# Routing three of the last token tiles inside the attention loop, and the fourth among the last merges

## The chip, the cores and the metric

The kernel runs on one core of one Trainium2 chip. The time is that of one execution on the device, in microseconds; the figure given is the median of several runs. Five engines work beside each other, each through its own queue in order: TensorE (PE, with its weight loads shown as PEld), VectorE (DVE), ScalarE (ACT), GpSimd (POOL) and SyncE (SP), which here issues most transfers.

## The reference

Three stages follow each other on 1152 tokens (2 sequences of 576) of 512 features:

```python
scores = 0.125 * q @ k.T                      # 2 x 8 heads, 576 x 576, head_dim 64
kth = np.partition(scores, -32)[..., -32]     # only the 32 largest of a row count
attn = softmax(where(scores >= kth, scores, -1e9))
x = (attn @ v)                                # -> 1152 x 512

logits = x @ w_gate                           # 8 experts
e = argmax(logits); gate = softmax(logits)[e]
# token i is the counts[e]-th of its expert; dropped if counts[e] >= capacity (288)
y = relu(x_e @ w1[e]) @ w2[e]                 # per expert
x = gate * y

h = x @ w_in
out = (h * clip(h + 3, 0, 6) / 6) @ w_out     # 512 -> 2048 -> 512
```

A token's place in its expert's list depends on all tokens before it, so the routing of a tile of 128 tokens needs the choices of the earlier tiles.

## The kernel before, in words

The tokens are cut into nine tiles of 128 (0 to 8), each with eight heads: 72 units `u`, eight to a tile. `in_steps` runs a software pipeline over 73 steps `i`; in one step each unit is at another stage. `STEP`, a string of letters, is the order written out by hand in which the stages are put into the queues: R is the first-round maxima of unit i+1 (`round1`, eight MAX8 on VectorE) interleaved with the merge of unit i-3 (`merge`, the 32 largest, seven dependent operations); G is `rest` (norm of half a tile, gate logits, routing, and the `judge` operations on POOL); L is `round2` of unit i-2 (L360); X, C and B are `excess` (POOL, L348), `cut_excess` (ScalarE, L353) and `drop_excess` (POOL, L356), which prepare what `round2` reads; S, Z and M are `shift` (POOL, L385), `shift_rest` (ScalarE) and `below` (ScalarE, L394); T is `ptr` (five pairs of transposing matmuls on TensorE, L408 and L409), E the exponential `expo` (ScalarE), A the product `attv` (TensorE, L426). `part` and `mask` are VectorE's versions of `shift` and `below`, used behind the loop. Buffers of `excess` (s2) are three, of the transposed scores in PSUM (`pt`) one.

Routing has parts: `pick` (L465 to L470, five VectorE operations), `weigh` (an exponential), `count` (small matmuls that number the tokens of an expert, then a copy to SBUF), and `weight + place` (L486 to L494, seven VectorE operations), whose result `dest` is the row in the DRAM tensor `xs`. `ROUTES` says which tiles are routed together, in which step, and how many steps lie between two sends: tiles 0 to 3 in step 41, sent every sixth step; tiles 4 to 7 in step 71. `pick` is put into step `at`, the placing into step `at + 1`. The second group's placing is put in once in step 72 and once more behind the loop. `scatter` scales a tile's rows on ScalarE (L518) and sends them by an indirect DMA from POOL's queue (L140).

The first expert's 192 rows do not wait for all tokens: rows of tiles 0 to 6 are read back from `xs` by `load_first` (two DMAs on SP's queue, L188 and L189) and turned by TensorE (`x_rows`, L166), and those of tiles 7 and 8 are added by a matmul with a matrix of ones and zeros (`x_pick`, L173, with the matrix `pick0` that VectorE makes) into the same two PSUM banks, which are then copied to `xe0`. Behind that come eight experts (L819) and the feed-forward stage. `keep_warm` is a number of matmuls on zeros whose result is not used (L566).

Of the kernel before, what the change touches and what calls it, by code (L numbers as in the profile page):

```python
# [8 lines left out]
F32 = mybir.dt.float32  # L9
# [9 lines left out]
P = 128  # L19
# [3 lines left out]
NT = 9  # L23
NU = NT * H
# [20 lines left out]
KW = 11  # L45
FILL = 4
MIX = {1: (0, 0), 3: (0, 1), 5: (0, 2), 7: (0, 3), 11: (1, 0), 15: (1, 1), 19: (1, 2), 23: (1, 3)}
ROUTES = ((0, 4, 41, 6), (4, 8, 71, 1))
VS = D + 9
VC = 96  # L50
MC = 96
# [6 lines left out]
def topk_attention_moe_ffn_kernel(ctx, tc, qT, kT, vx, vT, wg, w1, w2, w_in, w_out, out, cap):  # L58
    nc = tc.nc
# [18 lines left out]
    def forward(fast):  # L78
# [79 lines left out]
        def x_copy(xp, g, x):  # L158
            nc.vector.tensor_copy(x[:, 2 * g:2 * g + 2, :W], xp[:, :, :W])

        def x_rows(xp):
            for g in range(2):
                for i in range(2):
                    ks = slice((2 * g + i) * P, (2 * g + i + 1) * P)
                    for r, r0, n in ((x0, 0, P), (x0b, P, W - P)):
                        nc.tensor.matmul(xp[g][:, i, r0:r0 + n], r[:, ks], ident[:n, :n], is_transpose=True,  # L166
                                         start=False, stop=False)

        def x_pick(xp, xg, t, start=False, x=None):
            for g in range(2):  # L170
                for i in range(2):
                    ks = slice((2 * g + i) * P, (2 * g + i + 1) * P)
                    nc.tensor.matmul(xp[g][:, i], xg[:, ks], pick0[t], start=start and i == 0,  # L173
                                     stop=x is not None and i == 1)
                if x is not None:
                    x_copy(xp[g], g, x)
# [14 lines left out]
        with ExitStack() as actx:  # L191
# [137 lines left out]
            def interleave(*chains):  # L329
                chains = [list(c) for c in chains]  # L330
                n = max([1] + [len(c) for c in chains])
                for i in range(n):
                    for ops in chains:
                        for f in ops[i * len(ops) // n:(i + 1) * len(ops) // n]:
                            f()
# [22 lines left out]
            def round2(u):  # L358
                t, h = divmod(u, H)
                nc.vector.max(lists[t % 2][:, h, NCK], st2.pop(u))  # L360
# [200 lines left out]
            def in_steps():  # L561
                wm = ps_t.tile([P, 8, P], F32, name="pt").rearrange("p a b -> p (a b)")[:, :512]

                def keep_warm(n, out):
                    for _ in range(n):
                        nc.tensor.matmul(out, dummy[:, :P], dummy, start=True, stop=True)  # L566

                def rest(i):
                    t, h = divmod(i - 4, H)
                    tn, hn = divmod(i - LAG, H)  # L570
                    if t >= 0 and h == H - 1:
                        judge(t)
                    interleave(norm(tn, hn - 3, hn + 1) if tn >= 0 and hn % 4 == 3 else [],
                               gate(tn - 1) if tn > 0 and hn == 0 else [],
                               *[routes[at][3 * (i - at)] for _, _, at, _ in ROUTES if i in (at, at + 1)])

                def issue(u):
                    if u % 2 == 0:
                        if u % H == 0 and 2 < u // H + 2 < NT:
                            load_q(u // H + 2)  # L580
                        scores(u, u + 1)

                routes = {}
                sent = 0
                blocks = {"X": (0, excess), "C": (1, cut_excess), "B": (1, drop_excess), "L": (2, round2), "S": (3, shift),
                          "Z": (3, shift_rest), "M": (3, below), "T": (4, ptr), "E": (4, expo), "A": (5, attv)}
                keep_warm(KW, wm)
                issue(0)
                for u in range(2):
                    fetch(u)  # L590
                interleave(round1(0))
                issue(2)
                fetch(2)
                for i in range(NU + 1):
                    for a, b, at, _ in ROUTES:
                        if i == at:
                            routes[at] = route(a, b)
                    if i == 16:
                        for name in stream[:2]:
                            load_w(name)  # L600
                        clear_rows(zero)
                    for o in STEP:
                        if o == "R":
                            interleave(round1(i + 1) if i + 1 < NU else [], merge(i - 3) if i >= 3 else [])
                        elif o == "G":
                            rest(i)
                        elif o == "F":
                            if i + 3 < NU:
                                fetch(i + 3)
                        elif o == "Q":  # L610
                            if i % 2 == 0 and i + 4 < NU:
                                issue(i + 4)
                            if i in MIX:
                                mix(*MIX[i])
                            if i < 4:
                                keep_warm(FILL, wm)
                        elif o == "V":
                            if i - 1 in MIX:
                                mixed(*MIX[i - 1])
                        elif 0 <= i - blocks[o][0] < NU:  # L620
                            blocks[o][1](i - blocks[o][0])
                    for a, b, at, gap in ROUTES:
                        if i == at:
                            routes[at][1]()
                            routes[at][2]()
                        n, r = divmod(i - at - 2, gap)
                        if r == 0 and 0 <= n < b - a:
                            scatter(a + n)
                            sent = a + n + 1
                mine = {t: big.tile([P, 1], F32, name=f"mine{t}") for t in xg_last}  # L630

                def pick(t):
                    nc.vector.scalar_tensor_tensor(mine[t], pos[:, t, 0:1], 1.0, oh[:, t, 0:1], op0=OP.add, op1=OP.mult)
                    nc.vector.tensor_scalar(pick0[t], slot1, mine[t], None, op0=OP.is_equal)

                u = NU - 1
                round2(u)
                interleave(merge(u - 1), merge(u), norm(NT - 1, 0, 4), routes[NU - 1][3])
                spare = ps_s.tile([P, 2, 512], F32, name="ps")[:, 0]
                warm = lambda n: keep_warm(n, spare)  # L640
                send = lambda t: scatter(t) if t >= sent else None
                for f, *args in ((ptr, u - 2), (expo, u - 2), (attv, u - 3), (send, 4), (send, 5), (attv, u - 2),
                                 (warm, 5), (part, u - 1), (below, u - 1), (part, u), (mask, u), (ptr, u - 1),
                                 (expo, u - 1), (send, 6), (load_first,), (scale, 7, xg_last[7]), (warm, 5), (ptr, u),
                                 (attv, u - 1), (pick, NT - 2), (expo, u), (judge, NT - 1), (warm, 1), (attv, u)):
                    f(*args)

                t = NT - 1
                banks = [pool.tile([P, 2, 512], F32, name=name)[:, 0, :2 * W].rearrange("p (a w) -> p a w", a=2)
                         for pool, name in ((ps_s, "ps"), (ps_t, "pt"))]  # L650
                interleave(norm(t, 4, H))
                x_pick(banks, xg_last[NT - 2], NT - 2, True)
                interleave(gate(t))
                nc.scalar.copy(plain.rearrange("p (h d) -> p h d", d=D), x_tok[:, t, :, :D])
                route_now(t, NT, lambda pos, tot: [
                    lambda: nc.vector.scalar_tensor_tensor(mine[t], pos[:, 0, 0:1], 1.0, oh[:, t, 0:1], op0=OP.add,
                                                           op1=OP.mult),
                    lambda: nc.vector.tensor_scalar(pick0[t], slot1, mine[t], gates[:, t], op0=OP.is_equal,
                                                    op1=OP.mult),
                    *most(tot)])  # L660
                x_rows(banks)
                send_rows(NT - 2, xg_last[NT - 2])
                x_pick(banks, plain, t, False, xe0)
                warm(WARM[1])
                nc.scalar.activation(xg_last[t], plain, AF.Copy, scale=gates[:, t])
                send_rows(t, xg_last[t])
# [355 lines left out]
```

## Time and profile before

| | us |
|---|---|
| median of 3 runs | 641.39 (641.07 to 641.99) |
| profiled execution | 639.62 |
| its span in the trace | 637.8 |
| PE busy in the span | 609.8 (96%) |
| DVE busy | 375.5 (59%) |
| ACT busy | 360.3 (56%) |
| POOL busy | 311.3 (49%) |

The profile is of one execution. Times in its rows count from the start of the span. Busy shares over the whole span are means over stages with different limits: the attention loop until about 234 us, its tail until 254 us, the experts until 428 us, the feed-forward stage until the end.

### The profile page before, as it was taken

To read this page: it belongs to the slowest core of one execution; us is meant where nothing else is said; L and a number is where in the kernel's file an instruction comes from. 1 tells how busy PE (TensorE), PEld (TensorE's weight loads), DVE (VectorE), ACT (ScalarE), POOL (GpSimd) and SP (SyncE) were. 2 spreads that over 40 slices of the span, in tenths; PEclk is the share of its full clock that TensorE was granted. 3 is DMA by queue.
4 is the path that set the end of the run, shared out by engine and by line. 5 is a ranking of instruction groups with operands and counts; after the bars stand their busy time and mean duration, and the time that the engine had idled before them with its cause. 6 is when DMAs were issued, how large, how long until landed. Compare 5 with 4: busy or idle time off the path is not lost.

```text
span 637.8 us, 12077 instructions
## 1 busy us (share of the span) xinstructions
PE 609.8 (96%) x4096; PEld 549.2 (86%) x4096; DVE 375.5 (59%) x1765; ACT 360.3 (56%) x687; POOL 311.3 (49%) x380
## 2 busy tenths in 40 slices
PE   8999999999888879999999999999999999999994
PEld 4888889888777767999999999999999999999993
DVE  5999999999999994002333323427665664222220
ACT  5999999989999963121334334336555553242221
POOL 7999999979999953001244222124234322030001
PEclk9999999999999979999999999999999999999998
DMA  8549600100000002885889887422222310020001
GB/s 268 168 134 386 212 17 2 35 2 18 18 18 19 2 1 95 293 290 148 306 264 280 276 308 239 165 64 85 81 85 84 97 34 1 1 99 1 1 1 54
DMA packets 36598, 74.13 MB, mean 116 GB/s; under 512 B 4016, under 2 KB 12464, under 8 KB 36528
## 3 DMA queue, kind: packets, MB, share of 16 engines
q1 hardware_dynamic: 34800, 68.55, 32.7%
q0 software_dynamic: 1728, 4.72, 2.0%
q8 instruction: 34, 0.56, 0.3%
q14 instruction: 36, 0.29, 0.2%
HBM read 63.83 MB, written 9.44 MB: 115 GB/s over the span
## 4 chain that ended last, share of the span: by engine, by line
PE 52%; DVE 24%; issue 15%; POOL 6%; ACT 1%; DMA 1%; DVEq 0%; SPq 0%; POOLq 0%; ACTq 0%
PE hps L819 13%; PE yps L819 13%; PE h L916 8%; PE acc L930 7%; DVE lists L342 7%; DVE lists L360 5%; DVE l L369 4%; DVE tops L371 3%; PE av L426 2%; POOL s L356 2%; PE ps L321 2%; PE pt L408 2%; POOL out_dram L939 1%; PE pt L566 1%; PE mix L443 1%
## 5 line engine op out<-in xcount | busy, mean ns | idle before, releaser
L342 DVE MAX8 lists<-s 128x8 f32<-128x72 f32 x576 | 118.6, 220 | 4.1 <-ACT s L326 4.1
L426 PE MATMUL av<-vt,pts 128*128 128x96 f32 (+1 forms) x800 | 100.5, 275 | 0.0
L916 PE MATMUL h<-x2h,fw 128*128 128x384 f32 x384 | 98.3, 336 | 0.9 <-DVE x2l L837 0.9
L426 PEld LDWEIGHTS av<-vt,pts 128*128 128x128 f32 (+1 forms) x800 | 92.1, 184 | 2.1 <-issue 0.9
L356 POOL TENSOR_TENSOR s<-s,cut 128x576 f32<-128x576 f32 x72 | 92.0, 1277 | 3.6 <-ACT cut L353 3.5
L819 PE MATMUL yps<-hT,wslot 128*128 128x192 f32 x512 | 90.9, 326 | 0.0
L930 PE MATMUL acc<-fw,gh 128*128 128x512 f32 x288 | 89.6, 392 | 0.0
L348 POOL TENSOR_TENSOR s<-s,lists 128x576 f32<-128x576 f32 x72 | 83.6, 1162 | 6.1 <-DVE lists L342 3.8
L408 PE MATMUL pt<-ident,ub 128*128 128x128 f32 x360 | 72.6, 287 | 13.5 <-POOL ub L385 7.9
L819 PE MATMUL hps<-xe,wslot 128*128 128x192 f32 x512 | 84.6, 326 | 0.2 <-DVE sc L184 0.2
L819 PEld LDWEIGHTS hps<-xe,wslot 128*128 128x128 f32 x512 | 83.4, 190 | 0.7 <-issue 0.7
L819 PEld LDWEIGHTS yps<-hT,wslot 128*128 128x128 f32 x512 | 82.1, 190 | 1.2
L408 PEld LDWEIGHTS pt<-ident,ub 128*128 128x128 f32 x360 | 50.8, 141 | 33.6 <-POOL ub L385 16.4
L916 PEld LDWEIGHTS h<-x2h,fw 128*128 128x128 f32 x384 | 70.5, 188 | 5.1 <-DVE x2l L837 1.2
L409 PE MATMUL pt<-drop,lb 128*128 128x128 bf16 x360 | 65.7, 220 | 0.0
L916 PE MATMUL h<-x2l,fw 128*128 128x384 f32 x192 | 64.7, 337 | 0.0
L930 PEld LDWEIGHTS acc<-fw,gh 128*128 128x128 f32 x288 | 53.4, 188 | 9.0
L919 ACT ACTIVATE g<-h,three 128x384 f32<-128x384 f32 x48 | 27.9, 581 | 55.7 <-PE h L916 55.7
L920 DVE SCALAR_TENSOR_TENSOR g<-g,h 128x384 f32<-128x384 f32 x48 | 26.5, 551 | 54.3 <-ACT g L919 53.9
L394 ACT ACTIVATE lb<-s,tops 128x576 bf16<-128x576 f32 x71 | 55.0, 775 | 4.9 <-DVE tops L371 2.8
L924 DVE TENSOR_TENSOR gl<-g,gh 128x384 fp32r<-128x384 f32 x48 | 27.4, 571 | 51.0 <-ACT gh L923 51.0
L923 ACT CAST gh<-g 128x384 fp32r<-128x384 f32 x48 | 24.7, 515 | 57.5 <-PE acc L930 52.9
(393 smaller groups left out, 1057.2 us busy)
## 6 DMA issues: line engine op xcount, KB each, us to landing
wslot<-in_w_dram SPq DMA_DIRECT2D x15, 2048.0 KB, 9.3
raw<-in_w_in_dram SPq DMA_DIRECT2D x16, 512.0 KB, 5.0
raw<-in_w_out_dram SPq DMA_DIRECT2D x16, 512.0 KB, 3.6
xs<-x_tok SPq DMA_DIRECT2D x8, 576.0 KB, 13.1
vt<-in_vx_dram SPq DMA_DIRECT2D x8, 365.0 KB, 3.6
kt<-in_kT_dram SPq DMA_DIRECT2D x8, 288.0 KB, 4.5
vts<-in_vT_dram SPq DMA_DIRECT2D x8, 288.0 KB, 3.8
qt<-in_qT_dram SPq DMA_DIRECT2D x9, 256.0 KB, 4.2
```

The lines of the kernel that those rows point to most:

```text
L342: yield lambda c=c: nc.vector.max(lists[t % 2][:, h, c], st[u][:, c * CW:(c + 1) * CW])
L348: nc.gpsimd.tensor_tensor(s2, s, lists[t % 2][:, h, :NCK, KEEP:].to_broadcast([P, NCK, CW]), op=OP.subtract)
L356: nc.gpsimd.tensor_tensor(st2[u], st[u], cuts.pop(u), op=OP.subtract)
L360: nc.vector.max(lists[t % 2][:, h, NCK], st2.pop(u))
L394: nc.scalar.activation(lbufs[u % 2][:, :S], st.pop(u), AF.Relu, bias=tops[t][:, h, TOPK - 1:], scale=-1.0)
L408: nc.tensor.matmul(pt[:, c], ubufs[u % 2][:, cs], ident, is_transpose=True, start=True, stop=False)
L409: nc.tensor.matmul(pt[:, c], lbufs[u % 2][:, cs], drop, start=False, stop=True)
L426: nc.tensor.matmul(av[t, g][rows, h % 4], pts[:, c, cols], vt[b, h // 2][:, at:at + VC], start=c == 0, stop=c == 4)
L819: nc.tensor.matmul(out, wb[:, k], m[:, k], start=first and k == 0, stop=last and k == HP - 1)
L916: nc.tensor.matmul(h2, fw[f][:, 0, a, k * P:(k + 1) * P], (x2h, x2l)[b][:, k, c * CH:(c + 1) * CH], start=n == 0, stop=n == len(ops) - 1)
L919: nc.scalar.activation(g, h2, AF.Relu, bias=three)
L930: nc.tensor.matmul(acc[j], g[a][:, j * P:(j + 1) * P], fw[f][:, 1, b], start=f == 0 and n == 0, stop=f == NF - 1 and n == 2)
```

## The change

Tiles 4 to 6 are routed in step 63, their rows are sent in the steps 65, 66 and 67, and the read-back is put behind step 69. Tile 7 is routed alone behind the loop: its `pick` is interleaved with the merge of unit 71, the rest follows the last mask. The two last merges are no longer interleaved with each other. The row transposes move ahead of the last attention product and now clear the banks; both banks come from one PSUM tile. Two groups of five warming matmuls are gone, and so is the second placing.

```diff
-ROUTES = ((0, 4, 41, 6), (4, 8, 71, 1))
+ROUTES = ((0, 4, 41, 6), (4, 7, 63, 1))
+FIRST = 69
...
-        def x_rows(xp):
+        def x_rows(xp, start):
             for g in range(2):
                 for i in range(2):
                     ks = slice((2 * g + i) * P, (2 * g + i + 1) * P)
                     for r, r0, n in ((x0, 0, P), (x0b, P, W - P)):
                         nc.tensor.matmul(xp[g][:, i, r0:r0 + n], r[:, ks], ident[:n, :n], is_transpose=True,
-                                         start=False, stop=False)
-
-        def x_pick(xp, xg, t, start=False, x=None):
+                                         start=start and i == 0 and r0 == 0, stop=False)
+
+        def x_pick(xp, xg, t, x=None):
             for g in range(2):
                 for i in range(2):
                     ks = slice((2 * g + i) * P, (2 * g + i + 1) * P)
-                    nc.tensor.matmul(xp[g][:, i], xg[:, ks], pick0[t], start=start and i == 0,
+                    nc.tensor.matmul(xp[g][:, i], xg[:, ks], pick0[t], start=False,
                                      stop=x is not None and i == 1)
...
                         if r == 0 and 0 <= n < b - a:
                             scatter(a + n)
-                            sent = a + n + 1
+                    if i == FIRST:
+                        load_first()
...
-                u = NU - 1
-                round2(u)
-                interleave(merge(u - 1), merge(u), norm(NT - 1, 0, 4), routes[NU - 1][3])
-                spare = ps_s.tile([P, 2, 512], F32, name="ps")[:, 0]
-                warm = lambda n: keep_warm(n, spare)
-                send = lambda t: scatter(t) if t >= sent else None
-                for f, *args in ((ptr, u - 2), (expo, u - 2), (attv, u - 3), (send, 4), (send, 5), (attv, u - 2),
-                                 (warm, 5), (part, u - 1), (below, u - 1), (part, u), (mask, u), (ptr, u - 1),
-                                 (expo, u - 1), (send, 6), (load_first,), (scale, 7, xg_last[7]), (warm, 5), (ptr, u),
-                                 (attv, u - 1), (pick, NT - 2), (expo, u), (judge, NT - 1), (warm, 1), (attv, u)):
+                u, t = NU - 1, NT - 1
+                wm, xp = (ps_s.tile([P, 2, 512], F32, name="ps") for _ in range(2))
+                warm = lambda n: keep_warm(n, wm[:, 0])
+                banks = [xp[:, g, :2 * W].rearrange("p (a w) -> p a w", a=2) for g in range(2)]
+                pick_e, weigh, count, place, _ = route(t - 1, t)
+                interleave(merge(u - 1), norm(t, 0, 4))
+                for f in (shift, shift_rest, below):
+                    f(u - 1)
+                for f, *args in ((ptr, u - 2), (expo, u - 2), (attv, u - 3), (round2, u)):
                     f(*args)
-
-                t = NT - 1
-                banks = [pool.tile([P, 2, 512], F32, name=name)[:, 0, :2 * W].rearrange("p (a w) -> p a w", a=2)
-                         for pool, name in ((ps_s, "ps"), (ps_t, "pt"))]
+                interleave(merge(u), pick_e)
+                for f, *args in ((weigh,), (part, u), (mask, u), (ptr, u - 1), (expo, u - 1), (attv, u - 2), (count,),
+                                 (ptr, u)):
+                    f(*args)
+                interleave(place)
+                for f, *args in ((pick, t - 1), (expo, u), (attv, u - 1), (x_rows, banks, True), (scale, t - 1, xg_last[t - 1]),
+                                 (judge, t), (warm, 1), (attv, u)):
+                    f(*args)
                 interleave(norm(t, 4, H))
-                x_pick(banks, xg_last[NT - 2], NT - 2, True)
+                x_pick(banks, xg_last[t - 1], t - 1)
...
-                x_rows(banks)
                 send_rows(NT - 2, xg_last[NT - 2])
-                x_pick(banks, plain, t, False, xe0)
+                x_pick(banks, plain, t, xe0)
                 warm(WARM[1])
```

## Rows read from the trace of the kernel before

**Rows 1.** Stretches: start:end, length, busy PE, PEld, DVE, ACT, POOL, PEclk, DMA, GB/s.
```profile
220.00:230.00 10.00, 6.71 (x65) 6.15 (x65) 9.66 (x53) 7.78 (x13) 10.00 (x12) 1.00 0.01 2
230.00:240.00 10.00, 8.30 (x68) 7.71 (x68) 9.52 (x56) 5.45 (x10) 2.19 (x4) 0.66 0.00 0
...
254.40:427.60 173.20, 173.00 (x1081) 171.49 (x1081) 50.50 (x118) 55.56 (x142) 39.07 (x43) 1.00 0.74 242
427.60:637.80 210.20, 201.22 (x1008) 181.84 (x1008) 91.37 (x156) 84.99 (x156) 47.43 (x44) 0.99 0.15 47
```

**Rows 2.** Chain of work that ended last: start, length, what; 244 to 255 us.
```profile
244.27 2.72 DMA xs<-xg,dest
...
247.39 2.98 DMA wslot<-xs
...
250.41 0.73 PE ps L166 x3
...
254.41 10.64 PE hps L819 x64
```

**Rows 3.** Timeline, all engines: start, length, engine, line, operation [idle before <-releaser]; 231 to 252 us.
```profile
231.80 0.23 DVE L367 MAX8 tops<-lists 128x8 f32<-128x63 f32 x1
...
233.69 0.17 DVE L486 TENSOR_REDUCE gt<-el 128x4 f32<-128x32 f32 x1
...
234.76 1.41 DVE L360 MAX8 lists<-s 128x8 f32<-128x576 f32 x2
...
240.17 0.51 DVE L402 TENSOR_SCALAR lb<-s,tops 128x576 bf16<-128x576 f32 x1
...
243.44 0.14 PEld L408 LDWEIGHTS pt<-ident,ub 128*128 128x128 f32 x1 [0.27 <-ACT pts L415]
...
244.30 1.20 PEld L426 LDWEIGHTS av<-vt,pts 128*128 128x128 f32 x10
...
247.00 0.16 DVE L432 TENSOR_SCALAR rs<-av 128x4 f32<-128x4 f32 x1 [5.77 <-PE av L426]
...
249.81 0.38 DVE L658 TENSOR_SCALAR wslot<-wslot,mine,gates 128x192 f32<-128x192 f32 x1
...
251.99 0.62 PEld L173 LDWEIGHTS ps<-wslot 128*128 128x128 f32 x4
```

**Rows 4.** Timeline of POOL alone, 137 to 231 us.
```profile
137.18 0.32 POOL L377 TENSOR_TENSOR over<-lists 128x64 f32<-128x64 f32 x1
...
142.96 1.16 POOL L140 DMA_INDIRECT xs<-xg,dest  x1 [1.48 <-DVE tops L371]
...
198.57 1.27 POOL L356 TENSOR_TENSOR s<-s,cut 128x576 f32<-128x576 f32 x1
...
201.07 1.17 POOL L348 TENSOR_TENSOR s<-s,lists 128x576 f32<-128x576 f32 x1
...
209.60 1.16 POOL L348 TENSOR_TENSOR s<-s,lists 128x576 f32<-128x576 f32 x1
...
228.62 0.51 POOL L385 TENSOR_TENSOR ub<-tops,s 128x200 f32<-128x200 f32 x1
229.10 1.26 POOL L356 TENSOR_TENSOR s<-s,cut 128x576 f32<-128x576 f32 x1
```

**Rows 5.** Timeline of VectorE alone, 130 to 231 us.
```profile
130.87 1.12 DVE L466 TENSOR_TENSOR dl<-L,mx 128x32 f32<-128x32 f32 x1
...
136.15 1.10 DVE L491 TENSOR_SCALAR rd<-cm 128x4 f32<-128x4 f32 x1
...
203.99 0.76 DVE L360 MAX8 lists<-s 128x8 f32<-128x576 f32 x1 [0.29 <-POOL s L356]
206.83 0.76 DVE L360 MAX8 lists<-s 128x8 f32<-128x576 f32 x1
...
228.53 1.89 DVE L466 TENSOR_TENSOR dl<-L,mx 128x32 f32<-128x32 f32 x1
...
230.45 0.19 DVE L467 SCALAR_TENSOR_TENSOR cand<-dl,desc 128x32 f32<-128x32 f32 x1
```

More of the change, by code (lines that the diff above doesn't have):

```diff
@@ L583, in in_steps @@
                 routes = {}
-                sent = 0
                 blocks = {"X": (0, excess), "C": (1, cut_excess), "B": (1, drop_excess), "L": (2, round2), "S": (3, shift),
```

## The prediction

> **What bounds the kernel now.** First I read the busy times by stretch [rows 1]. From 254.40 us on the expert stage holds TensorE busy for 173.00 of 173.20 us, and in the feed-forward stage it is busy for 201.22 of 210.20 us, the drain at the end included: whatever moves the first expert matmul moves the end by as much. The change lies wholly before that matmul, so the question is when it starts; it starts at 254.41 [rows 2]. In the last part of the attention loop, 220 to 230 us, the tight engine is another one: POOL 10.00 of 10 us, VectorE 9.66, TensorE only 6.71 [rows 1].
>
> Second, the chain that ended last [rows 2]: the send of tile 6's rows leaves POOL at 244.27 and takes 2.72 us to land, the read-back takes 2.98 us more, at 250.41 the rows are in, and their transposes run until tile 8's own picks can start at 251.99 [rows 3]. Third, the tail in time order [rows 3]: the pick matrix of tile 8, the other input of those picks, was made by VectorE at 249.81 + 0.38 = 250.19. So the read-back chain is late by only 251.99 - 250.25 = 1.74 us against a parallel chain (last attention product, norm, gate, routing of tile 8) that the change leaves in place. That is all that the removal of the two transfers can give.
>
> **The change part by part.** I use two marks. T is the start of the second-round maximum of unit 70 (L360, step 72): 234.76 now [rows 3]. N is the start of the last norm: 247.00 now, T + 12.24 [rows 3].
>
> *Sends and read-back out of the tail.* The transfers then lie some 14 us ahead of their use (last send in step 67, read-back behind step 69; from the send's start to the rows' arrival it was 250.41 - 244.27 = 6.1 us [rows 2]). After N nothing else changes: pick matrix at N + 3.19, picks at N + 3.25, and from the picks to the first expert matmul 254.41 - 251.99 = 2.42 us as now. Gain at equal N: 1.74 us. Both PSUM banks now come from one tile; I take the copy of one bank and the matmuls of the other as independent, at nothing (if not, a copy of some 0.6 us is added).
>
> *Sends into the loop.* POOL is the bound there and has no idle time from 201.07 to 230.36. One send costs it 201.07 - (198.57 + 1.27) = 1.23 us, gap to gap [rows 4]; with the memset and gaps I take 1.25. Three in the steps 65, 66 and 67 cost 3.75 us, less only what slack POOL has. Each also needs a scaling on ScalarE ahead of it. In step 43, right after a routing, the first send waited 1.48 us for that scaling [rows 4]; the order of work in step 65 is the same, ScalarE's `below` waits for VectorE's merge, then come the exponential and the scaling. I count 1.15 us for the first send (bounds 0 and 1.48), nothing for the next two, which POOL reaches later than ScalarE does. On the other queues: SP holds only the read-back and then the expert weights, which wait for the tail anyway. On ScalarE three scalings lie beside a POOL step of 4.1 us.
>
> *Routing into the loop, step 63.* VectorE gets there at 203.99 - 0.29 = 203.70 [rows 5]. There are five operations in step 63 and seven in step 64. An undisturbed one takes 0.19 us and a gap of 0.03 (230.45 [rows 5]). Two kinds are not undisturbed: the subtraction `dl` (L466), which reads two tiles of SBUF, and `rd` (L491). `dl` took 1.12 us in step 41 and 1.89 us in step 71 [rows 5]; the second one began at 228.53, POOL operations began at 228.62 and at 229.10, and it ended at 230.42, when the last one was over at 229.10 + 1.26 and POOL had nothing to do [rows 4, 5]. So it did not get in between two POOL operations that followed each other. In step 63 POOL runs without a gap until it is starved: its next `excess` (step 64) may start only when VectorE's L360 of step 63 is through, for s2 has three buffers. From 201.07 and 2.84 us a step (three steps to 209.60 [rows 4]) POOL runs dry at 206.75. I take `dl` until then; three more operations give L360 at 207.45 instead of 203.99, and its end, 208.2, starts POOL again. Step 64: first round and merge are 206.83 - 203.99 - 0.75 = 2.08 us [rows 5], to 210.3; three operations to 210.9; `rd` until POOL's operation is over at 211.1 (in step 42 it took 1.10 us [rows 5]); three more, and L360 of step 64, which I call X, starts at 211.7, now 206.83. Bounds: with no such wait at all 203.70 + 1.05, + 0.75 + 2.08, + 1.4 = 209.0; with `dl` at the one-operation price 210.4; with TensorE late with the position counts, as in step 41, 212.2.
>
> The Trainium skill, "SBUF — State Buffer", section "Who interferes with whom", states that a VectorE instruction with two SBUF inputs and a GpSimd instruction that reads SBUF exclude each other, and that the one which issues first has the ports for its whole instruction. By that rule `dl` would wait for one POOL operation, and X would be the 210.4 of the second case; the 1.89 us of step 71 lies over two, so the trace agrees with the exclusion and not with the turn-taking.
>
> *What this makes of T.* POOL's `excess` of step 65 starts at X + 0.75. From there to the end of its last drop operation of the loop it has 229.10 + 1.26 - 209.60 = 20.76 us of gapless work now [rows 4]; with 3.75 and 1.15 added, T = X + 0.75 + 20.76 + 3.75 + 1.15 = X + 26.4 = 238.1. VectorE alone would be there earlier: from L360 of step 64 to T it needs 234.76 - 206.83 = 27.9 us now, but some 3.7 of these are the routing, of which it is rid. T is 3.35 us later than now. What leaves the loop in exchange is in these numbers: now VectorE does the routing in steps 71 and 72, which is why T comes 4.4 us after POOL's last operation.
>
> *The tail, T to N.* VectorE now runs two second rounds (1.41 us), both merges together with norm and a repeated placing, two shifts, a mask, until 240.68, T + 5.92 [rows 3]. After the change: second round 0.71, merge of 70 with norm 2.25 (a merge alone takes 233.69 - 231.80 = 1.89 us [rows 3]; what is put between its dependent steps adds little), second round 0.71, merge of 71 with tile 7's pick 2.1, mask 0.51 and a shift of about that length: T + 6.8. The last transposes `ptr` then start at T + 6.9 (now 243.44, T + 8.7, held by the exponential of unit 70 and by a TensorE at half clock in part of 230 to 240 us [rows 1, 3]). Behind them on TensorE: 0.86 us for themselves, 1.2 us for the product of unit 70 [rows 3], the row transposes that have moved here, 8/7 of 251.99 - 250.41 = 1.8 us [rows 2, 3], and 247.00 - 245.50 = 1.5 us for one warming matmul and the last product: N = T + 12.26. So what the two dropped groups of five warming matmuls and the shorter wait give, the row transposes take. I count 0 for the tail, bounds -0.5 and +1.0.
>
> *Sum.* +3.35 + 0.0 - 1.74 = +1.6 us. The profiled execution took 639.62 us, 1.82 around its span of 637.8, and lies 1.77 below the median of 641.39; I add the difference to either: 641.2 profiled, 643.0 as the median.
>
> **The rivals.**
>
> *One operation's wait (641.7).* `dl` gets in at the next boundary of POOL, 203.95, and the next two-input operations each at a boundary; L360 of step 63 is at 205.9, POOL is not starved there, X = 210.4, T = 236.8, +2.05 - 1.74 = +0.3. For it: `rd` of step 42 ended at 137.25 although POOL went on at 137.18 [rows 4, 5]. Against it: step 71's `dl`.
>
> *Covered after all (639.2, faster).* The routing slips in without a wait and the first scaling is ready before POOL has done its step: X = 209.0, T = 209.75 + 20.76 + 3.75 = 234.26, 0.5 earlier than now; -0.5 - 1.74 = -2.2. It is decided by whether POOL's `excess` of step 65 starts before 210 us. For it: VectorE waits 0.29 us for POOL at 203.99, so there is a little room, and the repeated placing is gone. Against it: the waits of steps 41, 42, 43 and 71, every routing that the trace shows.
>
> *Half clock in the tail (645.9).* The granted clock was 0.66 on average in 230 to 240 us, so it was at the lower of its two levels (1.2 instead of 2.4 GHz) for some two thirds of them, behind the routing of step 71, whose count TensorE had to wait for; with 6.71 of 10 us busy before that it was full [rows 1]. With ten warming matmuls gone, a drop there would run the last `ptr`, two products and the row transposes at about 1.6 times their 5 us: +2.9, so +4.5. Against it: by my order TensorE has no hole over 1 us between T and N.
>
> **How the numbers follow.** Forecast (643.0, of its own 642.2 to 644.4) 0.40; one operation's wait 0.27; covered 0.20; half clock 0.13. A change within 0.2% (1.3 us) can't be told from none here. The first case falls with some 0.06 of its 0.40 into the middle, the second with 0.25 of 0.27; the fourth is slower whole, the third faster for nearly all. Faster 0.20, same 0.32, slower 0.48. For the range I leave out the end of the third case and most of the fourth: 639.5 to 645.2.
>
> **What would show it.** In the new trace: `dl` in step 63 (L466) over 2 us long, ending with POOL's operation near 206.7; L360 of step 64 near 211.7; the three sends close together with one idle gap ahead of the first; T near 238.1; row transposes between the products of unit 70 and 71, some 1.8 us, without a wait for a transfer; the first expert matmul at N + 5.7, near 256.0. Wrong would be: T at or before 236, or N - T a microsecond off 12.2, or a clock under 1.0 behind T.

## The result, and the profile after

The changed kernel takes 644.39 us in the median (643.32 to 647.5, seven executions) against 641.54 for the kernel before in the same comparison: ratio 1.0057, 95% interval 1.0043 to 1.0072 (the two medians alone give 1.0044). It is slower, by about 2.9 us where +1.6 were forecast. The profiled execution took 646.27 us with a span of 644.3, so it is one of the longer ones, and the trace shows why.

VectorE first, in time order (start, length, engine, line, operation; lines are one later here, L467 is `dl`, L361 is what L360 was). It answers to [rows 5] and, with the last two lines, to T and N of [rows 3].

```profile
202.02 0.75 DVE L361 MAX8 lists<-s 128x8 f32<-128x576 f32 x1
...
205.04 3.01 DVE L467 TENSOR_TENSOR dl<-L,mx 128x24 f32<-128x24 f32 x1
208.09 0.18 DVE L468 SCALAR_TENSOR_TENSOR cand<-dl,desc 128x24 f32<-128x24 f32 x1
...
208.62 0.75 DVE L361 MAX8 lists<-s 128x8 f32<-128x576 f32 x1
...
211.65 0.71 DVE L488 TENSOR_SCALAR gt<-gt 128x3 f32<-128x3 f32 x1
...
213.03 0.75 DVE L361 MAX8 lists<-s 128x8 f32<-128x576 f32 x1
...
239.73 0.76 DVE L361 MAX8 lists<-s 128x8 f32<-128x576 f32 x1
...
251.80 0.16 DVE L433 TENSOR_SCALAR rs<-av 128x4 f32<-128x4 f32 x1 [3.86 <-PE av L427]
```

The first line is L361 of step 62, which the change can't have moved. In the trace before it was this one:

```profile
200.78 0.76 DVE L360 MAX8 lists<-s 128x8 f32<-128x576 f32 x1
```

This execution was thus 1.24 us late before the change began, and from here on I measure from that line, R. Step 64's L361, X, is at R + 11.01 (before R + 6.05), T at R + 37.71 (before 33.98), N at T + 12.07 (before 12.24).

POOL in time order, with its idle time before an operation and what ended it; it answers to [rows 4].

```profile
205.15 1.15 POOL L349 TENSOR_TENSOR s<-s,lists 128x576 f32<-128x576 f32 x1
206.27 0.51 POOL L386 TENSOR_TENSOR ub<-tops,s 128x200 f32<-128x200 f32 x1
206.75 1.26 POOL L357 TENSOR_TENSOR s<-s,cut 128x576 f32<-128x576 f32 x1
209.45 1.16 POOL L349 TENSOR_TENSOR s<-s,lists 128x576 f32<-128x576 f32 x1 [1.44 <-DVE lists L361]
...
213.86 1.16 POOL L349 TENSOR_TENSOR s<-s,lists 128x576 f32<-128x576 f32 x1 [1.53 <-DVE lists L361]
...
218.23 0.99 POOL L141 DMA_INDIRECT xs<-xg,dest  x1 [1.46 <-DVE lists L343]
...
222.32 0.98 POOL L141 DMA_INDIRECT xs<-xg,dest  x1 [0.17 <-ACT cut L354]
...
227.26 1.01 POOL L141 DMA_INDIRECT xs<-xg,dest  x1 [0.16 <-ACT s L327]
```

POOL runs dry twice at the routing and once ahead of the first send, as forecast. The row of that send names a VectorE operation as the last signal; the scaling that it also needs ended on ScalarE at 217.96, 0.27 us ahead of it. In the trace before, tile 6's send follows its scaling by as much (243.39 + 0.62 = 244.01, then 244.27), so I take the scaling as what the first send waited for.

```profile
217.25 0.71 ACT L519 ACTIVATE xg<-x_tok,gates 128x512 f32<-128x512 f32 x1
```

Behind N the chain that ended last does not go as forecast (start, length, what; it answers to [rows 2]):

```profile
255.13 0.98 PE ps L174 x4
256.13 0.57 DVE xe L160
...
256.75 1.65 PE ps L174 x4
258.39 1.29 PE ps L567 x3
...
259.78 12.05 PE hps L822 x64
```

The picks of the second bank start only behind the copy of the first, and they take 1.65 us where four took 0.98; three warming matmuls (L567) then end last of all that the first expert waits for, and its 64 products take 12.05 us where they took 10.64 [rows 2]. The stretches tell why (columns as in [rows 1]; the last but two is the granted clock):

```profile
254.00:255.00 1.00, 0.39 (x10) 0.30 (x9) 0.89 (x6) 0.65 (x2) 0.00 (x0) 1.00 0.00 0
255.00:256.00 1.00, 0.86 (x4) 0.62 (x4) 0.68 (x6) 0.24 (x1) 0.00 (x0) 0.91 0.00 0
256.00:257.00 1.00, 0.35 (x2) 0.26 (x2) 0.56 (x1) 0.00 (x0) 0.47 (x1) 0.50 0.00 0
...
262.00:264.00 2.00, 2.00 (x12) 2.00 (x11) 0.00 (x0) 0.33 (x1) 0.00 (x0) 0.84 1.06 390
```

From 255.8 to 262.6 us TensorE had half its clock (1.2 of 2.4 GHz). Ahead of that it had waited twice for the routing of tile 8, with only small matmuls between:

```profile
254.01 0.17 PE L479 MATMUL pos_p<-oh,tri 128*128 128x8 bf16 x1 [0.74 <-DVE oh L471]
...
255.13 0.96 PE L174 MATMUL ps<-wslot 128*128 128x192 f32 x4 [0.73 <-DVE sums L515]
```

### The profile page after: what moved, and what is told of

Same layout as the page of the kernel before. It is cut to its first block, busy times and chain, and to the rows that moved or that the text cites. A ratio compares the mean times of both kernels' runs of the same rounds, so it can differ in the third digit from the quotient of the medians.

```text
span 644.3 us, 12069 instructions
## 1 busy us (share of the span) xinstructions
PE 614.6 (95%) x4086; PEld 552.2 (86%) x4086; DVE 378.7 (59%) x1769; ACT 361.8 (56%) x690; POOL 312.4 (48%) x381
## 4 chain that ended last, share of the span: by engine, by line
PE 48%; DVE 26%; issue 15%; POOL 6%; ACT 2%; POOLq 0%; DVEq 0%; ACTq 0%
PE hps L822 13%; PE yps L822 13%; DVE lists L343 9%; PE h L919 8%; PE acc L933 7%; DVE lists L361 6%; DVE l L370 5%; DVE tops L372 3%; POOL s L357 2%; PE av L427 2%; POOL s L349 1%; POOL out_dram L942 1%; DVE tops L368 1%; DVE x_tok L435 1%; PE xp L154 1%
## 5 line engine op out<-in xcount | busy, mean ns | idle before, releaser
L409 PE MATMUL pt<-ident,ub 128*128 128x128 f32 x360 | 74.2, 291 | 13.9 <-POOL ub L386 9.0
L822 PE MATMUL hps<-xe,wslot 128*128 128x192 f32 x512 | 86.0, 330 | 0.1
L822 PEld LDWEIGHTS hps<-xe,wslot 128*128 128x128 f32 x512 | 84.8, 193 | 1.0 <-issue 1.0
L410 PE MATMUL pt<-drop,lb 128*128 128x128 bf16 x360 | 67.1, 223 | 0.0
L933 PE MATMUL acc<-fw,gl 128*128 128x512 f32 x144 | 57.1, 396 | 0.0
```

The costliest lines, as they stand in the source:

```text
L409: nc.tensor.matmul(pt[:, c], ubufs[u % 2][:, cs], ident, is_transpose=True, start=True, stop=False)
L410: nc.tensor.matmul(pt[:, c], lbufs[u % 2][:, cs], drop, start=False, stop=True)
L822: nc.tensor.matmul(out, wb[:, k], m[:, k], start=first and k == 0, stop=last and k == HP - 1)
L933: nc.tensor.matmul(acc[j], g[a][:, j * P:(j + 1) * P], fw[f][:, 1, b], start=f == 0 and n == 0, stop=f == NF - 1 and n == 2)
```

## The experiments

All marks of the profiled executions, in us: X, T from R; N from T; H, the first expert matmul, from N; the 64 products that follow; and the end of these from R against before (64.27). Ratios are against the kernel before in the same comparison, whose median was 641.54 for the changed kernel, 641.11 for e1 to e4, 641.17 for e5 to e8 and 641.59 for e9 and e10. Executions also differ outside these marks, whatever the change: R lies between 200.76 and 202.28, and what follows the 64 products takes 372.5 to 374.0 us. So a median need not follow the end mark of one profile within 1 us. The code cuts below are shortened.

| | X | T | N | H | 64 | end | median | ratio (95%) |
|---|---|---|---|---|---|---|---|---|
| before | 6.05 | 33.98 | 12.24 | 7.41 | 10.64 | 0 | 641.5 | |
| changed | 11.01 | 37.71 | 12.07 | 7.98 | 12.05 | +5.54 | 644.39 | 1.0057 (1.0043 to 1.0072) |
| e1 two tiles | 11.01 | 37.72 | 12.06 | 5.73 | 10.64 | +1.88 | 644.26 | 1.0050 (1.0036 to 1.0064) |
| e2 fill | 11.01 | 37.72 | 12.06 | 6.65 | 10.64 | +2.80 | 643.93 | 1.0038 (1.0023 to 1.0053) |
| e3 rows late | 11.03 | 37.75 | 10.27 | 9.45 | 11.56 | +4.76 | 644.38 | 1.0047 (1.0034 to 1.0060) |
| e4 sends out | 11.02 | 34.99 | 10.56 | 9.62 | 11.39 | +2.29 | 643.26 | 1.0020 (1.0004 to 1.0037) |
| e5 two tiles, fill | 11.02 | 37.71 | 12.07 | 5.73 | 10.64 | +1.88 | 643.17 | 1.0028 (1.0017 to 1.0038) |
| e6 e4, two tiles, fill | 11.01 | 34.99 | 10.91 | 6.72 | 10.64 | -1.01 | 640.02 | 0.9984 (0.9975 to 0.9993) |
| e7 split rows | 11.02 | 35.01 | 10.93 | 5.80 | 10.64 | -1.89 | 639.09 | 0.9973 (0.9964 to 0.9983) |
| e8 before, fill | 6.05 | 33.98 | 12.42 | 7.64 | 10.64 | +0.41 | 640.19 | 0.9990 (0.9980 to 0.9999) |
| e9 pick behind | | 35.94 | 10.54 | 5.79 | 10.64 | -1.36 | 639.79 | 0.9970 (0.9957 to 0.9983) |
| e10 no warm(1) | 11.03 | 35.02 | 10.36 | 5.80 | 10.64 | -2.45 | 638.60 | 0.9955 (0.9943 to 0.9967) |

**e1, the banks in two tiles.**

```diff
-wm, xp = (ps_s.tile([P, 2, 512], F32, name="ps") for _ in range(2))
-banks = [xp[:, g, :2 * W]... for g in range(2)]
+banks = [ps_s.tile([P, 2, 512], F32, name="ps")[:, 0, :2 * W]... for _ in range(2)]
+spare = ps_t.tile([P, 8, P], F32, name="pt")   # for the warming matmuls
```

> The two PSUM banks of the first expert's rows come from two tiles again, one bank each, and the warming matmuls go to the transposes' tile; all else as in the changed kernel. Theory 1 (the loss is in the loop: routing and three sends beside a full POOL make T, the start of L360 of unit 70, some 3.5 us later; the tail after the last norm costs nothing but one serial copy): the picks of the second bank start right behind those of the first instead of behind the copy, 0.65 us less from the last norm to the first expert matmul, T unchanged; some 0.6 us faster than the changed kernel (about 642.9 in its quicker executions), still slower than the kernel before. Rival 2 (most of the loss is made behind the last norm, by the shared tile and by TensorE falling to its lower clock because it waits there): 2 us or more come back, 641.5 or less, and the lower clock is gone.

The chain that ended last, in e1: all eight picks in one piece, then the second copy.

```profile
253.88 1.55 PE ps L174 x8
255.45 0.56 DVE xe L160
...
256.27 10.64 PE hps L828 x64
```

Neither theory had all of it. In the profiled execution T is unmoved and H is at N + 5.73, so up to there the loss is +1.88, near the forecast's +1.6. But the median is no better than the changed kernel's, and the executions reach from 642.48 to 645.21; the profiled one is the shortest, and no trace shows what the longer ones lost. It kept full clock behind N although it has the same two waits as the changed kernel:

```profile
252.76 0.17 PE L479 MATMUL pos_p<-oh,tri 128*128 128x8 bf16 x1 [0.74 <-DVE oh L471]
...
253.88 1.38 PE L174 MATMUL ps<-wslot 128*128 128x192 f32 x7 [0.73 <-DVE sums L515]
```

**e2, the holes filled.**

```diff
 x_pick(banks, xg_last[t - 1], t - 1)
+warm(2)
...
 send_rows(NT - 2, xg_last[NT - 2])
+warm(3)
 x_pick(banks, plain, t, xe0)
```

> The changed kernel with two warming matmuls behind the picks of tile 7 and three ahead of the picks of tile 8, in holes in which TensorE waits for the routing of tile 8 (0.74 and 0.73 us in the trace). Theory 1: the median hardly moves against the changed kernel's quicker executions (643.5); only the long executions (646 to 647.5), which ran the first expert at the lower clock, are gone, and the granted clock behind the last norm is 1.00 in the profile. Rival 2: all of the loss behind the last norm is the clock, so the kernel comes to 641.5 or below.

The same chain, in e2: at full clock, but with the copy between the picks.

```profile
254.80 0.90 PE ps L174 x4
255.72 0.57 DVE xe L160
...
256.34 0.93 PE ps L174 x4
257.29 0.56 DVE xe L160
...
258.11 10.64 PE hps L824 x64
```

As theory 1 had it: five executions lie between 643.33 and 644.35 and none at 646 (a sixth took 2411.33 us, whose cause is not shown; the ratio leaves it out). H is at N + 6.65, 0.92 us behind e1, and behind e5, which differs from e2 only in the tiles: that is the price of the shared tile.

**e3, the row transposes put back behind the totals**, with `start=True` in the picks of tile 7 as in the kernel before.

> The changed kernel with the row transposes put back to where the kernel before has them, behind the totals of tile 8's routing. From the row transposes' 1.7 us ahead of the last attention product in the trace: the last norm comes 1.7 us earlier after T (10.3 instead of 12.05); behind it TensorE has holes of 0.74 and 0.73 us that take part of them, so the picks of tile 8 start some 1.0 us later after the norm; together 0.7 us faster than the changed kernel. If TensorE's idle holes behind the norm are what brings the lower clock, the long executions also go. Rival: the transposes were free ahead of the last product (the exponential of unit 71 is the later one), then the norm does not move and this is 1 us slower.

The norm came 1.8 us earlier, as expected. Of that, 1.47 us were lost again up to H (9.45 against 7.98), and the median is that of the changed kernel: the whole group lies between 644.0 and 645.4. The profiled execution fell to half clock at the picks of tile 8 and ran them and 11.56 us of products with it. That it would free the clock was wrong.

**e4, the sends behind the loop**, on top of e3.

```diff
-scatter(a + n)                 # tiles 4 to 6 in the steps 65, 66, 67
-if i == FIRST: load_first()
+if 69 <= i < 72: held[i - 65] = ...; scale(i - 65, held[i - 65])
...
+for n, xg in held.items(): scat.append(send_rows(n, xg))   # behind shift, shift_rest, below
+load_first()
```

> As e3, but the rows of tiles 4 to 6 are scaled in the steps 69 to 71 and sent behind the loop, one after the other, with the read-back behind them; the routing stays in step 63. Theory 1: POOL loses 3 x 1.25 us of sends and the 1.46 us wait for the first scaling, VectorE is then the bound of the loop's end, and T comes 2.4 us earlier than in e3; the read-back arrives about T + 11.5 and the row transposes need it at T + 13: some 2.4 us faster than e3, near 640.5, faster than the kernel before. Rival 2 (sends in the loop are hidden, the loss is in the tail): T stays where e3 has it, and the time is that of e3 or more, since the read-back is late again.

T is 2.76 us earlier than in e3: the three sends and the wait for the first scaling are worth that, and rival 2 is out. The time fell into two groups, three executions at 639.62 to 640.01 and nine at 643.04 to 644.2. The profiled one is of the upper group; its stretches (columns as in [rows 1]):

```profile
248.00:250.00 2.00, 1.26 (x23) 1.00 (x22) 1.69 (x11) 1.09 (x4) 1.09 (x2) 1.00 0.14 55
250.00:252.00 2.00, 2.00 (x9) 1.37 (x10) 1.07 (x7) 0.62 (x1) 0.08 (x1) 0.88 0.20 76
252.00:254.00 2.00, 1.35 (x5) 0.84 (x4) 0.56 (x1) 0.00 (x0) 0.89 (x1) 0.50 0.29 113
```

TensorE is at half clock from 251.5 us, behind a wait of 0.74 us for tile 8's routing that ended at 249.41, although the row transposes are back behind the totals.

**e5, e1 and e2 together.**

> The changed kernel with the two banks in two tiles (as e1) and the five warming matmuls in the holes behind the last norm (as e2). Theory: what the forecast left out is just these two, the copy that holds up the second bank's picks (0.92 us between e2's and e1's traces) and the lower clock of some executions. Then all executions lie close together, from the last norm to the first expert matmul it takes 5.7 us as forecast, and the time is that of the kernel before plus 1.9 (T + 3.73, the norm - 0.18, behind it - 1.68): ratio about 1.003. Rival: the executions still spread by 2 to 3 us or lie 3 us above the kernel before, then the lower clock was not what e1's median (3.1 above) was made of.

1.0028 is the ratio expected: with the tile and the clock mended, the changed kernel loses 1.88 us, and its executions lie within 642.3 to 643.8.

**e6, e4 with two tiles and three warming matmuls behind the picks of tile 7.**

> As e4 (sends behind the loop, row transposes behind the totals), with two tiles and three warming matmuls behind the picks of tile 7. From the traces of e4 and e1: T 1.0 us later than in the kernel before (the routing in the steps 63 and 64), the norm 1.7 us earlier after T, the first expert matmul 6.7 us behind the norm (now 7.4): 1.4 us faster than the kernel before, ratio about 0.998, and no execution in the upper group of e4 (643 to 644.2). Rival: e4's upper group has another cause than the clock behind the last norm; then two groups 3.4 us apart stay.

As expected, but for N, which came 1.33 us earlier after T where 1.7 were expected. e4's upper group is gone: eleven executions from 639.58 to 640.89. So I take that group as the clock behind N (two tiles alone had not brought e1's executions together).

**e7, the row transposes split.**

```diff
+x_rows(banks, (0,))      # behind x_pick(banks, xg_last[t - 1], t - 1, True), no warming matmuls there
...
-x_rows(banks)
+x_rows(banks, (1,))
```

> As e6, but instead of the three warming matmuls the first bank's four row transposes stand in the hole behind the picks of tile 7, the other four behind the totals. 0.9 us of real work fill a hole of 0.75 us, the count of tile 8 is 0.2 us later and the picks of tile 8 some 0.4 us earlier than in e6: 0.3 us faster than e6. If useful work keeps the clock as warming matmuls do, there is one group of executions.

Better than expected, 0.92 us from N to H, and one group: work that has to be done anyway keeps the clock as well.

**e8, the control.**

> Control: the kernel before with three warming matmuls behind the picks of tile 7 and three ahead of the row transposes, where TensorE waits for the routing and the read-back. If the kernel before does not fall to the lower clock behind the last norm, as its trace shows, this changes nothing: ratio 1.000 within 0.002. Rival: the kernel before has such executions too (its times reach from 639.8 to 642.4), then its median falls by 0.5 us or more and the comparison with the changed kernel was of two mixtures.

Between the two: 0.1% faster, barely outside no change. The profiled execution gained nothing: the kernel before had full clock behind N without the filling too. It is one of three at 641.49 to 641.99, apart from nine at 639.66 to 640.64, and lost its time elsewhere: behind the 64 products it took 373.8 us where the profile of the kernel before took 372.8. That the kernel before loses the clock now and then is possible, and was not seen in a trace.

**e9, the routing operations of steps 63 and 64 behind L361**, on top of e7.

> As e7, but the routing operations of the steps 63 and 64 stand behind L360 of their step instead of ahead of it. Then POOL does not run dry at the end of step 63: its next excess may start, and it stops only at the shift after that, which waits for a merge that is queued behind the routing. Theory (a VectorE operation with two SBUF inputs comes through only when POOL has stopped): the subtraction dl waits for that, about 3 us again, over three POOL operations, and ends with POOL's excess of step 64. Rival (it waits for one POOL operation, whichever has the ports): dl takes 1.2 us or less and the loop's end comes 1.5 to 2 us earlier than in e7.

VectorE (first fence) and POOL (second) of e9:

```profile
206.03 3.09 DVE L467 TENSOR_TENSOR dl<-L,mx 128x24 f32<-128x24 f32 x1
209.16 0.18 DVE L468 SCALAR_TENSOR_TENSOR cand<-dl,desc 128x24 f32<-128x24 f32 x1
```

```profile
206.22 0.51 POOL L386 TENSOR_TENSOR ub<-tops,s 128x200 f32<-128x200 f32 x1
206.69 1.26 POOL L357 TENSOR_TENSOR s<-s,cut 128x576 f32<-128x576 f32 x1
207.93 1.15 POOL L349 TENSOR_TENSOR s<-s,lists 128x576 f32<-128x576 f32 x1
210.62 0.52 POOL L386 TENSOR_TENSOR ub<-tops,s 128x200 f32<-128x200 f32 x1 [1.54 <-DVE l L370]
```

`dl` waited 3.09 us, past the start of three POOL operations, and ended at 209.12, when POOL's `excess` was over (207.93 + 1.15) and POOL had stopped. The theory holds for `dl`; the one-operation rival is out. T was 0.9 us later than in e7.

**e10, e7 without the last warming matmul.**

> As e7 without the one warming matmul ahead of the last attention product: in e6 and e7 it writes into the transposes' PSUM tile and so waits for the exponential of unit 71 to read it, and the last norm came 10.91 us behind T against 10.56 in e4. Expected: the norm at T + 10.3 to 10.6, 0.4 us faster than e7, ratio about 0.997 against the kernel before. Rival: the product waits for the same exponential anyway, then nothing changes.

The norm is at T + 10.36 as expected. The chain of e10 behind N:

```profile
247.62 1.33 PE ps L174 x8
248.95 0.78 PE ps L167 x4
249.72 0.29 PE pos_p L478 x8
...
250.04 0.23 PE tot_p L502 x9
250.27 0.84 PE ps L167 x4
251.11 1.51 PE ps L174 x8
...
253.46 10.64 PE hps L835 x64
```

TensorE has no hole left between the picks of tile 7 and those of tile 8. This version beats both kernels: 638.6 us, ratio 0.9955 against the kernel before.

## Why the prediction was right, and where it was short

**The gain of 1.74 us** from rows that are there in time was right in size: from N to H it is 5.73 us in e1 and e5 against 7.41 before, 1.68 less (forecast 5.67). The changed kernel did not get it (7.98), see below.

**Routing in step 63.** `dl` ended when POOL ran dry: 205.04 + 3.01 = 208.05, and POOL's last operation was over at 208.01. X came at R + 11.01, forecast 211.7 - 200.78 = 10.92. One detail was wrong: in step 64 it was not `rd` that waited but the addition ahead of it (L488, 0.71 us). The rival of one operation's wait fell for `dl`, here and in e9; `rd` of step 42, which came through although POOL went on [rows 4, 5], stays the one case against. The Trainium skill's rule in "SBUF — State Buffer", section "Who interferes with whom", that the instruction which issues first keeps the ports for that instruction, explains that `dl` waits; that it waited past three POOL operations in a row is more than the rule says, and the measurement decides.

**Sends in the loop.** The first waited 1.46 us (forecast 1.15), the others 0.17 and 0.16 as forecast. T came 3.73 us later than before, forecast 3.35; the difference is that wait (0.31 more) and X (0.09 more). e4 takes the 3.73 apart. 1.0 us is the routing: by the starts of L361 it makes the steps 63 and 64 4.97 us longer, where the steps 71 and 72 become only 3.77 us shorter (234.76 - 225.66 = 9.10 before, 236.63 - 231.30 = 5.33 in e4). 2.7 us are the sends and the wait. "Covered after all" fell with it: POOL's `excess` of step 65 started at 213.86 - 1.24 = 212.6 in the times of the trace before, not before 210.

**The tail, T to N**, forecast at 0 with N = T + 12.26, was 12.07, and T and N agree within 0.01 us in e1, e2 and e5, whatever else was changed.

**What failed** is the sentence "I take the copy of one bank and the matmuls of the other as independent, at nothing (if not, a copy of some 0.6 us is added)". They are not independent through one tile: the second bank's picks waited for the first bank's copy, 0.92 us (6.65 in e2 against 5.73 in e1), the copy and its two hand-overs.

**The half clock** was among the rivals with 0.13, at 2.9 us, but in the wrong place: between T and N TensorE stayed at full clock, as argued; behind N, where I said that nothing else changes, it fell. A clock under 1.0 behind T was one of the signs of being wrong, and it came. In the profiled execution that costs 7.98 - 6.65 = 1.33 us up to H and 12.05 - 10.64 = 1.41 in the products, 2.74 together; that this lies near the 2.9 is luck, for those were worked out for other work.

In the kernel before, row transposes had stood in the second of the two waits behind N; moved ahead of the last product, they left it empty. That their move brought the lower clock is not shown: e3 and e4 have them back in their old place and lost the clock in their profiles, and e1 has both waits empty and kept it. What is shown is what helps: with the first wait filled too, by warming matmuls (e2, e5, e6) or by half of the transposes (e7, e10), the long executions are gone. Why the kernel before, with the same 0.74 us empty, kept the clock in its profile stays open.

The sum then is 1.88 (forecast 1.6) + 0.92 + 2.74 = 5.54 us in the profiled execution. In the median it is 2.85, about the 2.80 that the sum gives without the clock, since not every execution lost it. That puts 644.39 at the upper edge of the forecast's own 642.2 to 644.4. With the two omissions mended, e5 took 643.17, where 643.0 was forecast.

## What to carry to other kernels

Work that is moved into a pipelined loop is priced by the engine that is full there: three sends of 1.25 us, with the wait for the first scaling, cost 2.76 us in the loop, and at most 0.3 us in the tail, where POOL idles (N from T, e4 against e3). Where a chain of small operations makes TensorE wait, put work into the hole that has to be done anyway: half of the row transposes there were worth 0.92 us against warming matmuls (e7 against e6). Two PSUM banks that are filled and copied in turn belong in two tiles.

## What the runs showed of the hardware

A half clock inside the loop cost nothing. In e1 (first fence) it was at the lower level from 208.8 to 215.6 us and in e2 (second fence) from 217.5 to 220.9, and X and T were the same within 0.02 us. In e1's rows TensorE was busy all of that time (2.00 of 2 us) and still not late; VectorE was busy for 1.93 to 2.00 of 2 us in all four rows.

```profile
208.00:210.00 2.00, 2.00 (x16) 1.95 (x15) 2.00 (x18) 1.80 (x4) 1.81 (x3) 0.69 0.01 4
...
214.00:216.00 2.00, 2.00 (x15) 1.81 (x14) 1.93 (x10) 1.44 (x4) 1.50 (x3) 0.60 0.00 0
```

```profile
216.00:218.00 2.00, 0.86 (x7) 0.79 (x8) 2.00 (x11) 2.00 (x4) 0.54 (x3) 0.87 0.02 4
...
220.00:222.00 2.00, 2.00 (x13) 1.34 (x12) 2.00 (x18) 2.00 (x4) 1.83 (x5) 0.78 0.06 21
```

And a VectorE subtraction of 24 elements a row took 3.01 to 3.09 us beside a POOL without gaps, where the operation behind it (L468), of the same size and also with two inputs, took 0.18 us with POOL idle.
